# Attention beside a long convolution: four channel blocks of 128 in place of two of 256, with complex butterflies in joint operations

## The chip, the cores and the metric

The kernel runs on one core of a Trainium2 chip. The metric is the device time of one execution in microseconds (us). Engines are named as the profile names them: PE is TensorE's matrix product, PEld its weight load, DVE is VectorE, ACT is ScalarE, POOL is GpSimd, and SP is the engine that issues most DMAs.

## The reference

Two independent parts share the output (2048 rows, 512 + 512 columns). Cut to what matters:

```
def _A_ref(x, wq, wk, wv, wo):            # 32 heads of 16, one K and V for all heads, S = 2048
    q = (x @ wq).reshape(B, S, H, Dh).transpose(0, 2, 1, 3)
    k = x @ wk
    v = x @ wv
    p = softmax(einsum("bhqd,bkd->bhqk", q, k) * Dh ** -0.5)
    return einsum("bhqk,bkd->bhqd", p, v).transpose(0, 2, 1, 3).reshape(B, S, H * Dh) @ wo

def _B_ref(q, k, v, shift_k, ssm_k, ssm_D):   # 512 channels
    k_shift = sum over t of k_pad[:, t:t + S, :] * shift_k[:, ks - 1 - t]      # 4 taps
    kv = k_shift * v
    y = irfft(rfft(kv, 2 * S) * rfft(ssm_k, 2 * S))[:S]    # causal convolution for each channel
    y = y + kv * ssm_D
    return q * y

return jnp.concatenate([a, b], axis=-1)
```

## The kernel before

**What sets the order.** The Python code emits one fixed order for each engine. It keeps three clocks of its own (`pe`, `act`, `dv`) and charges every operation an assumed price; nothing is scheduled at run time. `attend` walks through 1024 *turns*. A turn is one tile of scores (L1237: eight f16 matmuls in 64x32 tiles of the array) and one exponential on ScalarE over 128x1024 (L1244). Two score tiles fit in PSUM. Every second turn TensorE multiplies two finished tiles with the values (`pv`, L1274). In the other turn `fill` may emit *units* of side work: a unit is charged 216 ns and is a 512-column f16 step or a 128-column f32 step through all eight tiles of the array (L316). As many units are emitted as fit until 380 ns after the planned start of the exponential. So the chunks have one to three units.

**Jobs.** Side work comes as jobs, the one with the earliest due turn first. A job from `pair_job` has two phases that use opposite row halves; between them GpSimd clears a small tile (`tok`, L287) for which the second phase waits, and the planner leaves 1.1 us. All jobs write one PSUM tile F, so the next may start only when VectorE has evacuated the last. Other side work are the Q projections (`xT,wq`) and the output projection (`wo,o`).

**The convolution** is a transform of 2048 points in two steps, in f32. The first step, over 128 points, is a matrix product with tables (`ff`, back with `fi`); the second, over 16, is done on VectorE by `dft16`: two radix-4 passes (`dft4`) with twiddle factors between. For each block of 256 channels there are three kinds of stage. S (`short`) forms the four-tap convolution times v on VectorE and transforms it into the spectrum `cx`. L (`long`) transposes the filter (L606), evacuates it (L612) and transforms it into `ch`. VectorE then runs `dft16` on both, multiplies them (`product`, L445) and runs `dft16` back. B (`backward`) transforms back, multiplies by q (L655) and stores. Every forward job ends in an evacuation into the spectrum (L475). `DUE` gives the due turns of the stages, whose order is S0, L0, L1, B0, S1, B1. Table tiles come in a ring of four (`FT`), 128 KB for each half tile.

**VectorE's threads.** `run_dve` emits evacuations when the planner's clock has them ready, and in between the next operation of one of several Python generators. Each `yield 1215.0` is the assumed price in ns of the operation that follows. In the twiddles of `dft16` it reads `yield 360.0` before L419 and `yield 350.0` before L421 and L423.

**DMAs** go through SP's queue, one for each turn, or two with a long list. The planner assumes 6 us to landing. Reused buffers carry real semaphores.

Of the kernel before, what the change touches and what calls it, by code (L numbers as in the profile page):

```python
# [18 lines left out]
P = 128  # L19
# [4 lines left out]
CB = 256  # L24
# [21 lines left out]
DUE = {("S", 0): (60, 150), ("L", 0): (150, 300), ("L", 1): (380, 500), ("B", 0): (500, 560), ("S", 1): (560, 660), ("B", 1): (780, 860)}  # L46
# [71 lines left out]
class _Emit:  # L118
# [247 lines left out]
    def dft4(self, x, e):  # L366
        v = self.nc.vector
        add, sub = ALU.add, ALU.subtract
        re, im = (lambda t: t[:, 0]), (lambda t: t[:, 1])
        x0, x1, x2, x3 = x  # L370
        n = 1215.0

        def both(out, a, b, op):
            for part in (re, im):
                yield n
                v.tensor_tensor(part(out), part(a), part(b), op)  # L376

        yield from both(e, x0, x2, add)
        yield from both(x2, x0, x2, sub)
        yield from both(x0, x1, x3, add)  # L380
        yield from both(x3, x1, x3, sub)
        yield n
        v.tensor_tensor(re(x1), re(x2), im(x3), add)
        yield n
        v.tensor_tensor(im(x1), im(x2), re(x3), sub)
        yield n
        v.tensor_tensor(re(x2), re(x2), im(x3), sub)
        yield n
        v.tensor_tensor(im(x2), im(x2), re(x3), add)
        yield from both(x3, e, x0, sub)  # L390
        yield from both(x0, e, x0, add)

    def dft16(self, c, first, second, sign):
        v, w = self.nc.vector, self.w
        n = c.shape[-1]
        outer = lambda i: c[:, :, 4 * i : 4 * i + 4, :]
        inner = lambda i: c[:, :, i:16:4, :]
        e = w.tile([P, 2, 4, n], F32, tag="sp", name=self.nm("sp"))
# [7 lines left out]
        for ab in ((1, 1), (1, 2), (2, 1), (1, 3), (3, 1), (2, 3), (3, 2), (3, 3), (2, 2)):  # L406
            u = w.tile([P, 2, n], F32, tag="v2", name=self.nm("u"))
            x = c[:, :, row(*ab), :]
            ang = sign * 2 * np.pi * ab[0] * ab[1] / 16
            if ab == (2, 2):  # L410
                yield 230.0
                v.tensor_copy(u[:, 0], x[:, 0])
                yield 230.0
                v.tensor_scalar(x[:, 0], x[:, 1], -float(sign), None, ALU.mult)
                yield 230.0
                v.tensor_scalar(x[:, 1], u[:, 0], float(sign), None, ALU.mult)
            else:
                yield 360.0
                v.tensor_scalar(u, x, float(np.sin(ang)), None, ALU.mult)  # L419
                yield 350.0  # L420
                v.scalar_tensor_tensor(x[:, 0], x[:, 0], float(np.cos(ang)), u[:, 1], ALU.mult, ALU.subtract)  # L421
                yield 350.0
                v.scalar_tensor_tensor(x[:, 1], x[:, 1], float(np.cos(ang)), u[:, 0], ALU.mult, ALU.add)  # L423
# [7 lines left out]
    def product(self, cx, ch):  # L431
        for i in range(4):
            r = slice(4 * i, 4 * i + 4)
            t = self.w.tile([P, 2, 4, CB], F32, tag="sp", name=self.nm("t"))
            t = t[:, 0], t[:, 1]
            for out, a, b, op in (
                (t[0], cx[:, 0, r], ch[:, 0, r], ALU.mult),
                (t[1], cx[:, 1, r], ch[:, 1, r], ALU.mult),
                (ch[:, 1, r], cx[:, 0, r], ch[:, 1, r], ALU.mult),
                (ch[:, 0, r], cx[:, 1, r], ch[:, 0, r], ALU.mult),  # L440
                (cx[:, 0, r], t[0], t[1], ALU.subtract),
                (cx[:, 1, r], ch[:, 1, r], ch[:, 0, r], ALU.add),
            ):
                yield 1215.0
# [7 lines left out]
    def spectrum(self):  # L452
        return self.w.tile([P, 2, 16, CB], F32, tag="big", bufs=2, name=self.nm("sp"))

    def tables(self):
        seq = [("ff", 0)] * 2 + [("ff", 1), ("fi", 0), ("ff", 0), ("fi", 1)]
        self.tab = []
        for kind, _ in seq:
# [7 lines left out]
    def table(self, n):  # L466
        return lambda now: len(self.tab) > n

    def forward_job(self, n, m2, c, xs, inputs, due):

        ft, h, use = self.tab[n]
        pr = [([(ft[:, rho, q, :], xs[rho]) for rho in range(2)], 256 * q, CB) for q in range(2)]

        def out(F):
            self.nc.vector.tensor_copy(  # L475
                c[:, :, 2 * m2 : 2 * m2 + 2, :].rearrange("p q m n -> p m q n"), F.rearrange("p m (q n) -> p m q n", q=2)
            )

        j = self.pair_job(pr, [(1215.0, out)], due, [h] + inputs, f32=True)
        return j, use  # L480


    def conv_pe(self):
# [4 lines left out]
        yield from self.short(0, 0)  # L488
        yield from self.long(0, 8, *self.long_load(0))
        hin = self.long_load(1)  # L490
        yield lambda now: ("p", 0) in self.seen
        yield from self.long(1, 16, *hin)
        yield lambda now: ("b", 0) in self.seen
        yield from self.short(1, 32)

    def conv_back(self):
        for blk in range(2):
            yield lambda now: ("y", blk) in self.sp
            yield from self.backward(blk, 24 + 16 * blk)

    def conv_dve(self):
        nat = [0, 1, 2, 3]
        for blk, order in enumerate((("cx", "ch"), ("ch", "cx"))):
            for n in order:
# [9 lines left out]
    def short(self, blk, tab):  # L514
        nc, v = self.nc, self.nc.vector
        cs = slice(blk * CB, (blk + 1) * CB)
        kk = self.w.tile([P, 15, CB], F32, tag="in", name=self.nm("kk"))
        nc.gpsimd.memset(kk[0:1, 0:3, :], 0.0)
        taps = self.fetch([(kk[:, 11 + i, :], self.skd[i : i + 1, cs].broadcast_to([P, CB])) for i in range(4)], self.in_free)
        edge = [(kk[a:b, i, :], self.kr[a - 1 : b - 1, 13 + i, cs]) for i in range(3) for a, b in ((1, 16), (16, P))]  # L520
        k0 = self.fetch(edge, self.in_free)
        got = {r: self.fetch([(kk[:, r + 3, :], self.kr[:, r, cs])], self.in_free) for r in range(2)}
        vs = {}

        def load(m2):
            n = self.io()
            t = self.io_tile("va", (2, 2, CB))
            r = slice(2 * m2, 2 * m2 + 2)
            vs[m2] = n, t, self.fetch([(t[:, 0, i], self.vr[:, 2 * m2 + i, cs]) for i in range(2)])
# [3 lines left out]
        ends = []  # L533
        for m2 in range(8):
            if m2 == 0:
                yield self.room(self.io_users, IO)
                load(0)
            for r in range(2 * m2 + 2, 2 * m2 + 4):
                if r < 8:
                    got[r] = self.fetch([(kk[:, r + 3, :], self.kr[:, r, cs])], self.in_free)  # L540
            for r in range(3 + 2 * m2, 5 + 2 * m2) if 1 <= m2 < 4 else range(11, 16) if m2 == 4 else ():
                got[r, 1] = self.fetch([(kk[:, r - 5, :], self.kr[:, r, cs])], ends[min(3, (r - 5) // 2)])
            if m2 < 7:
                yield self.room(self.io_users, IO)
                load(m2 + 1)
            n, t, h = vs[m2]
            seg = (lambda r: r + 3) if m2 < 4 else (lambda r: r - 5)
            need = [h, taps] + ([k0] if m2 < 2 else [])
            need += [got[r] if m2 < 4 else got[r, 1] for r in range(2 * m2 - 3, 2 * m2 + 2) if m2 >= 4 or r >= 0]
            yield self.at(*need)  # L550
            a, tmp = t[:, 1], self.w.tile([P, 2, CB], F32, tag="v2", name=self.nm("t"))
            kx = lambda i: kk[:, seg(2 * m2 - i) : seg(2 * m2 - i) + 2, :]
            tap = lambda i: kk[:, 11 + i : 12 + i, :].broadcast_to([P, 2, CB])
# [7 lines left out]
            ends.append(Stamp(self.dv))  # L561
# [3 lines left out]
            yield self.table(tab + m2)  # L565
            j, use = self.forward_job(tab + m2, m2, c, [a[:, 0], a[:, 1]], [done], self.due("S", blk, m2))
            self.users(j, self.io_users[n], use)
            jobs.append(j)
        self.in_free = ends[-1]
        self.sp["cx", blk] = c, jobs  # L570

    def users(self, j, *stamps):

        j.uses = stamps

    def long_load(self, blk):
        hin = self.w.tile([P, 2, S], F32, tag="in", name=self.nm("hin"))
        hs = []
        for ct in range(2):
            c0 = blk * CB + ct * P  # L580
            hs.append(self.fetch([(hin[:, ct, x : x + 256], self.I["B_ssm_k"][c0 : c0 + P, x : x + 256]) for x in range(0, S, 256)], self.in_free))
        return hin, hs

    def long(self, blk, tab, hin, hs):
        nc = self.nc
        yield self.at(*hs)
        for ct in range(2):
            yield 100.0
            nc.vector.tensor_add(hin[:, ct, 0:1], hin[:, ct, 0:1], self.dt[:, 2 * blk + ct : 2 * blk + ct + 1])
        ready = Stamp(self.dv)  # L590
        hv = hin.rearrange("p c (q m) -> p c m q", m=16)
        c = self.spectrum()
        jobs = []
        for m4 in range(4):
            yield self.room(self.io_users, IO)
            n = self.io()
            t = self.io_tile("hT", (4, CB))

            def turn(m, m4=m4):
                def emit(F, most):  # L600
                    if most < 2:
                        return 0, None, False
                    for i in range(2):
                        for ct in range(2):
                            x = P * ct
                            nc.tensor.transpose(F[:, m, 256 * i + x : 256 * i + x + P], hv[:, ct, 4 * m4 + 2 * m + i], self.ident)  # L606
# [7 lines left out]
            j = self.one_job([turn(m) for m in range(2)], [(1215.0, out)], self.due("L", blk, 2 * m4), [ready])  # L614
            yield self.at(j)
            for i in range(2):
                m2 = 2 * m4 + i
                yield self.table(tab + m2)
# [1057 lines left out]
```

## Time and profile before

| what | value |
|---|---|
| median of 3 runs | 1005.43 us (1002.78 to 1006.14) |
| the profiled execution | 1007.34 us, its span 1005.6 us |
| granted TensorE clock, mean | 0.986 |
| first exponential to the end of the last | 19.2 to 990.0 us |
| data moved by DMA | 85.33 MB, mean 85 GB/s |

The profiled execution is 1.9 us above the median. A row of a group reads: line, engine, operation, output <- inputs with shapes, count | busy us in all, mean ns of one | idle time of the engine just before them, and what ended it. In a row of the timeline come the start in us, the length in us, the engine, the line, the operation, the names, the count of instructions merged, and in brackets the idle time before. An f32 matmul stands in the profile as two records.

### The profile page before, as it was taken

Reading aid. Unit: us, or ns where it says so; the run is one execution under the profiler, and the core shown is the slowest. Engines: PE = TensorE matmul, PEld = TensorE weight load, DVE = VectorE, ACT = ScalarE, POOL = GpSimd, SP = SyncE. Lnnn points to the kernel's source line nnn. Section 1 sums busy time; section 2 is a strip of 40 time slices with the busy share of each in tenths; the row PEclk is TensorE's granted clock in tenths of the full one; section 3 lists DMA queues with packets and bytes.
Section 4 is the critical chain, followed back from the end, with each engine's and each line's share of the span. In section 5 each row is a group of like instructions: output and inputs, shape, how many; then the busy total and the mean of one; then the engine's idle time right before and its main releaser. Section 6 shows DMA issues by size and latency. Waiting matters only on the chain.

```text
span 1005.6 us, 53610 instructions
## 1 busy us (share of the span) xinstructions
PE 947.9 (94%) x24556; PEld 483.1 (48%) x24556; DVE 652.6 (65%) x831; ACT 960.8 (96%) x1034; POOL 43.2 (4%) x106
## 2 busy tenths in 40 slices
PE   8999999999999999899999999999888998999996
PEld 4434444554545554354555555554333443455562
DVE  4334477736894998989869945464799989111322
ACT  4799999999999999999999999999999999999993
POOL 3820000000000000000000000000000000000000
PEclk8799999999999999999999999999999999999998
DMA  7133354244024212312145333332201021331201
GB/s 223 44 108 120 111 149 138 88 128 128 24 84 118 72 36 72 86 49 73 35 123 159 93 124 103 108 100 65 66 13 52 13 61 45 94 125 54 61 5 47
DMA packets 81941, 85.33 MB, mean 85 GB/s; under 512 B 14654, under 2 KB 70312, under 8 KB 81708
## 3 DMA queue, kind: packets, MB, share of 16 engines
q1 hardware_dynamic: 80076, 81.23, 27.1%
q8 instruction: 194, 3.18, 1.3%
q10 hardware_dynamic: 1632, 0.60, 0.3%
q14 instruction: 39, 0.32, 0.1%
HBM read 56.14 MB, written 25.66 MB: 81 GB/s over the span
## 4 chain that ended last, share of the span: by engine, by line
ACT 68%; issue 14%; PE 14%; DVE 3%; DMA 1%; ACTq 0%; SPq 0%; DVEq 0%
ACT p L1244 67%; PE a L1274 5%; PE s L1237 4%; PE f L316 1%; DMA xc<-in_A_x 1%; PE b L735 1%; DMA wkvf<-in_A_wv 1%; DVE u L419 1%; DVE sp L421 1%; PE s L728 1%; PE b L775 1%; DVE sp L475 0%; PE b L772 0%; DVE sp L423 0%; PE b L748 0%
## 5 line engine op out<-in xcount | busy, mean ns | idle before, releaser
L1244 ACT ACTIVATE p<-s 128x1024 f32<-128x1024 f32 x1016 | 946.1, 1046 | 12.9 <-PE s L1237 8.1
L1274 PE MATMUL a<-p,vx 64*32 64x512 f32 (+1 forms) x8640 | 547.8, 564 | 0.2 <-issue 0.2
L1237 PE MATMUL s<-st,kst 49*32 49x512 f16 x8192 | 428.8, 383 | 43.5 <-ACT p L1244 36.1
L1237 PEld LDWEIGHTS <-kst 49*32 49x32 f16 x8192 | 198.8, 89 | 376.4 <-issue 331.6
L1274 PEld LDWEIGHTS a<-p,vx 64*32 64x32 f32 x8640 | 168.0, 106 | 24.6 <-issue 2.8
L376 DVE TENSOR_TENSOR sp<-sp 128x1024 f32<-128x1024 f32 x96 | 111.2, 1214 | 0.0
L475 DVE COPY sp<-f 128x1024 f32<-128x1024 f32 x32 | 39.2, 1224 | 87.8 <-PE f L316 87.6
L376 DVE TENSOR_TENSOR sp<-sp,sp 128x1024 f32<-128x1024 f32 x48 | 56.1, 1216 | 0.3
L316 PE MATMUL f<-wo,o 64*32 64x512 f16 x1440 | 55.3, 375 | 0.1
L1290 DVE COPY ao<-a 128x1024 f32<-128x1024 f32 x15 | 18.4, 1224 | 54.6 <-PE a L1274 54.4
L316 PE MATMUL f<-xT,wq 64*32 64x512 f16 x1344 | 51.0, 375 | 0.1
L287 POOL MEMSET tok<- 1x2 f32 x58 | 5.6, 96 | 897.8 <-PE f L316 890.0
L655 DVE TENSOR_TENSOR q<-f,q 128x1024 f32<-128x1024 f32 x8 | 9.8, 1224 | 50.8 <-PE f L316 50.8
L316 PE MATMUL f<-va,ff 64*32 64x128 f32 (+1 forms) x1472 | 41.1, 311 | 0.2
L316 PE MATMUL f<-hT,ff 64*32 64x256 f32 (+1 forms) x1344 | 41.0, 325 | 0.0
L316 PE MATMUL f<-sp,fi 64*32 64x128 f32 (+1 forms) x1424 | 40.3, 315 | 0.0
L560 DVE TENSOR_TENSOR va<-va,t 128x512 f32<-128x512 f32 x48 | 33.2, 691 | 1.5
L316 PEld LDWEIGHTS f<-va,ff 64*32 64x32 f32 x1472 | 26.8, 106 | 15.3 <-issue 3.3
L558 DVE TENSOR_TENSOR t<-kk 128x512 f32<-128x512 f32 x48 | 33.0, 687 | 1.0
L316 PEld LDWEIGHTS f<-sp,fi 64*32 64x32 f32 x1424 | 26.4, 106 | 10.2 <-issue 3.0
L316 PEld LDWEIGHTS f<-hT,ff 64*32 64x32 f32 x1344 | 24.9, 106 | 12.8 <-DVE sp L475 2.7
L316 PEld LDWEIGHTS <-o 64*32 64x32 f16 x1440 | 23.2, 93 | 15.7 <-issue 4.2
(162 smaller groups left out, 569.4 us busy)
## 6 DMA issues: line engine op xcount, KB each, us to landing
ff<-in_ff SPq DMA_DIRECT2D x64, 128.0 KB
od<-ao SPq DMA_DIRECT2D x30, 256.0 KB
qd<-qp SPq DMA_DIRECT2D x45, 128.0 KB
st<-qd SPq DMA_DIRECT2D x60, 96.0 KB
kk<-in_B_k SPq DMA_DIRECT2D x38, 128.0 KB
va<-in_B_v SPq DMA_DIRECT2D x32, 128.0 KB
hin<-in_B_ssm_k SPq DMA_DIRECT2D x32, 128.0 KB
fi<-in_fi SPq DMA_DIRECT2D x32, 128.0 KB
```

Source lines behind the costliest of these rows:

```text
L316: last = self.nc.tensor.matmul(F[32 * q : 32 * q + 32, rho, cols + a : cols + b], w[rows, 32 * q : 32 * q + 32], x[rows, a:b], start=begin ...
L376: v.tensor_tensor(part(out), part(a), part(b), op)
L419: v.tensor_scalar(u, x, float(np.sin(ang)), None, ALU.mult)
L421: v.scalar_tensor_tensor(x[:, 0], x[:, 0], float(np.cos(ang)), u[:, 1], ALU.mult, ALU.subtract)
L475: self.nc.vector.tensor_copy(c[:, :, 2 * m2 : 2 * m2 + 2, :].rearrange("p q m n -> p m q n"), F.rearrange("p m (q n) -> p m q n", q=2))
L558: v.tensor_tensor(tmp, kx(i), tap(i), ALU.mult)
L560: v.tensor_tensor(a, a, tmp, ALU.add)
L728: self.nc.tensor.matmul(out[j : j + 32], w[:, j : j + 32], x, start=start, stop=stop)
L1237: self.nc.tensor.matmul(out, self.kst[rows, c0 : c0 + 32], x, start=True, stop=True)
L1244: i = self.nc.scalar.activation(p, self.s, AF.Exp, scale=DH**-0.5 / SC / SC)
L1274: nc.tensor.matmul(out, self.vx[rows, k, :], p, start=i == 0, stop=i == NK - 1)
L1290: self.nc.vector.tensor_copy(a, self.acc)
```

## The change

The block has 128 channels (`CB`) and there are four of them. A spectrum is half as large, and three stand in SBUF in place of two, so that the next block's S stage can start before the last block's B stage has run; the order of stages is S0 L0 S1 L1 B0 S2 L2 B1 S3 L3 B2 B3. A forward job covers four rows m with two table tiles where it covered two rows with one. A backward job still covers four rows m, which are now 8 units, and fills half of F. Each stage reads its 8 tables, so 96 table tiles are loaded in place of 48. The butterflies' plain sums take the real and the imaginary part in one operation, twiddles of equal angle go in pairs, and assumed prices change. Inputs and outputs of the convolution are fetched two rows at a time, in runs of 512 B. Some tiles of the start of the attention are placed in other buffers (`in`, `big`, `px`, `wo`).

The rows below are the engines' orders, each without its row number.

On VectorE, the first spectrum `cx`, the second `dft4` pass of its forward transform (`sp` is a spectrum, or the scratch tile of the pass when it stands alone as the output; `hT`, `f` and `rl` belong to other work). Before:

```order
L376 TENSOR_TENSOR sp_5234<-sp_1456 128x1024 x2
L612 COPY hT_5798<-f_6219 128x1024
L376 TENSOR_TENSOR sp_1456<-sp_1456 128x4x256 x5
L1367 TENSOR_SCALAR rl_6042<-rl_6042 128x32
L1369 RECIPROCAL rl_6042<-rl_6042 128x32
L376 TENSOR_TENSOR sp_1456<-sp_1456 128x4x256
L475 COPY sp_5250<-f_6330 128x2x2x256
L383 TENSOR_TENSOR sp_1456<-sp_1456 128x4x256
L385 TENSOR_TENSOR sp_1456<-sp_1456 128x4x256
L387 TENSOR_TENSOR sp_1456<-sp_1456 128x4x256
L389 TENSOR_TENSOR sp_1456<-sp_1456 128x4x256
L376 TENSOR_TENSOR sp_1456<-sp_5234,sp_1456 128x4x256 x2
```

Now:

```order
L375 TENSOR_TENSOR sp_3956<-sp_1462 128x1024
L375 TENSOR_TENSOR sp_1462<-sp_1462 128x8x128 x3
L383 TENSOR_TENSOR sp_1462<-sp_1462 128x4x128 x4
L473 COPY sp_3835<-f_4681 128x2x2x256
L386 TENSOR_TENSOR sp_1462<-sp_3956,sp_1462 128x8x128 x2
L1355 TENSOR_SCALAR rl_4643<-rl_4643 128x32
L1357 RECIPROCAL rl_4643<-rl_4643 128x32
```

A pass has 16 operations of 1024 elements before; now it has six of 1024 and four of 512, and there are twice as many passes.

On TensorE, the first chunk of the first S job, three units in both versions (`va` the short convolution's result, `ff` a table, `s` scores). Before:

```order
L1237 LDWEIGHTS kst
L1237 MATMUL s_2206<-st_1014,kst 32x512
L316 MATMUL f_2215<-va_1457,ff_354 32x256 x8
L316 MATMUL f_2215<-va_1457,ff_354 32x128 x8
L1237 LDWEIGHTS kst
L1237 MATMUL s_2235<-st_1014,kst 32x512
```

Now:

```order
L1225 LDWEIGHTS kst
L1225 MATMUL s_2203<-st_1020,kst 32x512
L318 MATMUL f_2212<-va_1463,ff_360 32x128
L318 MATMUL f_2212<-va_1463,ff_361 32x128
L318 MATMUL f_2212<-va_1463,ff_360 32x128
L318 MATMUL f_2212<-va_1463,ff_361 32x128
L318 MATMUL f_2212<-va_1463,ff_360 32x128
```

The chunk keeps its three units and its place between two score tiles; its 256-column matmuls have become pairs of 128 columns, and they read two tables in turn.

On SP, the first loads of the first S stage (`kk` the keys with the taps, `skd` the taps, 15 and 112 partitions for the rows before the first). Before:

```order
L178 DMA kk_1454<-skd 128x256 x4
L178 DMA kk_1454<-in_B_k 15x256
L178 DMA kk_1454<-in_B_k 112x256
L178 DMA kk_1454<-in_B_k 15x256
L178 DMA kk_1454<-in_B_k 112x256
L178 DMA kk_1454<-in_B_k 15x256
L178 DMA kk_1454<-in_B_k 112x256
L178 DMA kk_1454<-in_B_k 128x256 x2
L178 DMA va_1457<-in_B_v 128x256 x2
```

Now:

```order
L180 DMA kk_1460<-in_B_k 128x2x128 x2
L180 DMA kk_1460<-skd 128x4x128
L180 DMA kk_1460<-in_B_k 15x3x128
L180 DMA kk_1460<-in_B_k 112x3x128
L180 DMA va_1463<-in_B_v 128x2x128 x2
```

A piece keeps its 128 KB and is cut into rows half as long; taps and edge rows come in three pieces instead of ten.

The diff, cut to its core:

```diff
-CB = 256
+CB = 128
+NB = D // CB
-DUE = {("S", 0): (60, 150), ("L", 0): (150, 300), ("L", 1): (380, 500), ("B", 0): (500, 560), ("S", 1): (560, 660), ("B", 1): (780, 860)}
+STAGES = ("S0", "L0", "S1", "L1", "B0", "S2", "L2", "B1", "S3", "L3", "B2", "B3")
+DUE = dict(zip(STAGES, (60, 110, 170, 240, 300, 340, 400, 450, 490, 550, 620, 700)))
...
     def dft4(self, x, e):
-        def both(out, a, b, op):
-            for part in (re, im):
-                yield n
-                v.tensor_tensor(part(out), part(a), part(b), op)
-        yield from both(e, x0, x2, add)
...
+        for out, a, b, op in ((e, x0, x2, add), (x2, x0, x2, sub), (x0, x1, x3, add), (x3, x1, x3, sub)):
+            yield 1215.0
+            tt(out, a, b, op)
+        for out, a, b, op in (
+            (re(x1), re(x2), im(x3), add),
+            (im(x1), im(x2), re(x3), sub),
+            (re(x2), re(x2), im(x3), sub),
+            (im(x2), im(x2), re(x3), add),
+        ):
+            yield 690.0
+            tt(out, a, b, op)
+        for out, op in ((x3, sub), (x0, add)):
+            yield 1215.0
+            tt(out, e, x0, op)
...
-        for ab in ((1, 1), (1, 2), (2, 1), (1, 3), (3, 1), (2, 3), (3, 2), (3, 3), (2, 2)):
+        for a, b in ((1, 1), (1, 2), (1, 3), (2, 3), (3, 3), (2, 2)):
+            r = sorted({row(a, b), row(b, a)})
+            n = len(r)
...
-                yield 360.0
+                yield 150.0 + 135.0 * n
                 v.tensor_scalar(u, x, float(np.sin(ang)), None, ALU.mult)
-                yield 350.0
+                yield 150.0 + 135.0 * n
                 v.scalar_tensor_tensor(x[:, 0], x[:, 0], float(np.cos(ang)), u[:, 1], ALU.mult, ALU.subtract)
...
     def spectrum(self):
-        return self.w.tile([P, 2, 16, CB], F32, tag="big", bufs=2, name=self.nm("sp"))
+        return self.w.tile([P, 2, 16, CB], F32, tag="big", bufs=3, name=self.nm("sp"))
...
-    def forward_job(self, n, m2, c, xs, inputs, due):
-        ft, h, use = self.tab[n]
-        pr = [([(ft[:, rho, q, :], xs[rho]) for rho in range(2)], 256 * q, CB) for q in range(2)]
+    def forward_job(self, n, m4, c, xs, inputs, due):
+        tabs = self.tab[n - 1 : n + 1]
+        pr = []
+        for q in range(2):
+            for i in range(2):
+                pr.append(([(tabs[rho][0][:, i, q, :], xs[2 * rho + i]) for rho in range(2)], 256 * q + CB * i, CB))
...
+        for b in range(NB):
+            if b > 1:
+                yield lambda now: ("b", b - 2) in self.seen
+            yield from self.short(b)
+            if b:
+                yield lambda now: ("p", b - 1) in self.seen
+            yield from self.long(b)
...
-            j = self.pair_job(pr, [(1215.0, out)], self.due("B", blk, b), [tabs[0][1], tabs[1][1], h, st], f32=True)
+            j = self.pair_job(pr, [(700.0, out)], self.due("B", blk, b), [tabs[0][1], tabs[1][1], h, st], f32=True)
...
     def wo_heads(self):
-        yield lambda now: self.turn >= 60
+        yield self.at(self.xdh[3])
```

243 lines of the change are left out of this document (106 added, 137 removed).

## The prediction

> **What bounds the kernel now.** I read the page's busy line and its chain first, then the exponentials alone in order of time, then the stages.
>
> ```profile
> PE 947.9 (94%) x24556; PEld 483.1 (48%) x24556; DVE 652.6 (65%) x831; ACT 960.8 (96%) x1034; POOL 43.2 (4%) x106
> ...
> ACT 68%; issue 14%; PE 14%; DVE 3%; DMA 1%; ACTq 0%; SPq 0%; DVEq 0%
> ...
> L1244 ACT ACTIVATE p<-s 128x1024 f32<-128x1024 f32 x1016 | 946.1, 1046 | 12.9 <-PE s L1237 8.1
> ```
>
> ScalarE is busy 96% of the span with one kind of instruction, the 1024 exponentials of L1244, and they hold 68% of the chain. TensorE is close behind, VectorE is not (65%). The change touches no exponential, so it can pay or cost only through the distance from one exponential to the next. By stage (columns: stretch, then busy us and count of PE, PEld, DVE, ACT, POOL, then clock, DMA share, GB/s):
>
> ```profile
> 19.00:93.00 74.00, 72.36 (x1216) 32.53 (x1208) 29.21 (x59) 62.52 (x64) 33.38 (x34) 0.86 0.25 79
> ...
> 725.00:775.00 50.00, 40.28 (x872) 16.74 (x879) 47.59 (x64) 50.00 (x56) 0.00 (x0) 1.00 0.12 32
> ...
> 990.00:1005.60 15.60, 6.53 (x80) 2.14 (x64) 4.57 (x11) 0.00 (x0) 0.00 (x0) 0.76 0.11 39
> ```
>
> ```profile
> 93.00:990.00 897.00, 853.48 (x23168) 439.79 (x23161) 609.55 (x746) 891.36 (x961) 7.24 (x61) 1.00 0.28 82
> ```
>
> The start (64 exponentials in 74 us, TensorE busy 72 of it) and the end (15.6 us after the last one) belong to attention alone. The stretch between is where the convolution lies: 897 us, ScalarE busy 891. The exponentials there, merged wherever one follows the other without a gap (start, length, count, the gap before):
>
> ```profile
> 92.41 27.16 ACT L1244 ACTIVATE p<-s 128x1024 f32<-128x1024 f32 x29
> 119.81 59.26 ACT L1244 ACTIVATE p<-s 128x1024 f32<-128x1024 f32 x64 [0.23 <-PE f L316]
> 179.24 62.28 ACT L1244 ACTIVATE p<-s 128x1024 f32<-128x1024 f32 x67 [0.17 <-PE f L316]
> 241.72 41.38 ACT L1244 ACTIVATE p<-s 128x1024 f32<-128x1024 f32 x44 [0.20 <-PE s L1237]
> 283.58 186.38 ACT L1244 ACTIVATE p<-s 128x1024 f32<-128x1024 f32 x200 [0.48 <-PE s L1237]
> 470.73 68.34 ACT L1244 ACTIVATE p<-s 128x1024 f32<-128x1024 f32 x73 [0.78 <-PE s L1237]
> 539.27 59.36 ACT L1244 ACTIVATE p<-s 128x1024 f32<-128x1024 f32 x64 [0.20 <-ACT p L1244]
> 598.81 305.85 ACT L1244 ACTIVATE p<-s 128x1024 f32<-128x1024 f32 x330 [0.18 <-ACT p L1244]
> 905.47 70.53 ACT L1244 ACTIVATE p<-s 128x1024 f32<-128x1024 f32 x76 [0.82 <-PE s L1237]
> 976.50 13.47 ACT L1244 ACTIVATE p<-s 128x1024 f32<-128x1024 f32 x14 [0.50 <-PE s L1237]
> ```
>
> 961 exponentials in 897.56 us: 0.934 us each. The nine gaps sum to 3.56 us. The same view in a stage without any convolution or projection unit, and in a dense one:
>
> ```profile
> 725.09 48.85 ACT L1244 ACTIVATE p<-s 128x1024 f32<-128x1024 f32 x53
> ```
>
> ```profile
> 619.09 71.66 ACT L1244 ACTIVATE p<-s 128x1024 f32<-128x1024 f32 x77
> ```
>
> The last one of a row lasts its 1.05 us (the mean of L1244), so the pitch is (48.85 - 1.05)/52 = 0.919 without units and (71.66 - 1.05)/76 = 0.929 with them. At 0.919 throughout, 960 pitches would take 882.5 us: all that any placement of side work could give back is 897.6 - 1.05 - 882.5 = 14.0 us, gaps included.
>
> **The change, part by part.** TensorE. Each of the three kinds of stage has 128 units in both versions (a unit: 128 columns in f32 through all eight 64x32 tiles): 384 in all. Before, 119 pairs of units ran as one 256-column matmul and 146 units as 128 columns; now all 384 run as 128. What a 128-column unit costs:
>
> ```profile
> 514.55 0.65 PE L316 MATMUL f<-sp,fi 64*32 64x128 f32 x32
> 514.99 0.43 PE L1237 MATMUL s<-st,kst 49*32 49x512 f16 x8
> 515.21 0.86 PE L316 MATMUL f<-sp,fi 64*32 64x128 f32 x32
> ```
>
> Start to start: 32 records (two units, each matmul recorded twice) in 0.44 us, 0.22 a unit, and the eight f16 matmuls behind them 0.22. [...] The weights that are now loaded twice as often are hidden: 0 us.
>
> ```profile
> L316 PEld LDWEIGHTS f<-sp,fi 64*32 64x32 f32 x1424 | 26.4, 106 | 10.2 <-issue 3.0 <-DVE q L655 0.6 <-DVE sp L475 0.3
> ```
>
> [...]
>
> How the units fall between the scores is counted in the order: chunks of three units 119 before and 122 now, of two 138 and 124, of one 68 and 86, alternate gaps without any 100 and 94; the eight-matmul transposes 16 and 16. Up to turn 117 the chunks are the same. So the pitch stays: 0 us by count. The one shift is in place: stretches of 32 turns with 34 units or more go from eight to four, and the three without any go.
>
> VectorE. The rows for its forms:
>
> ```profile
> L376 DVE TENSOR_TENSOR sp<-sp 128x1024 f32<-128x1024 f32 x96 | 111.2, 1214 | 0.0
> ...
> L560 DVE TENSOR_TENSOR va<-va,t 128x512 f32<-128x512 f32 x48 | 33.2, 691 | 1.5
> ...
> L419 DVE TENSOR_SCALAR u<-sp 128x512 f32<-128x512 f32 x48 | 20.4, 426 | 1.4
> L421 DVE SCALAR_TENSOR_TENSOR sp<-sp,u 128x256 f32<-128x256 f32 x48 | 20.4, 425 | 1.6
> ...
> L412 DVE COPY u<-sp 128x256 f32<-128x256 f32 x6 | 1.8, 294 | 0.2
> ...
> L1491 DVE TENSOR_SCALAR lr<-lr 128x16 f32<-128x16 f32 x2 | 0.4, 185 | 0.1
> ```
>
> - Butterflies: 192 x 1.214 = 233 us before; 144 x 1.214 + 96 x 0.691 = 241 now: +8. Joining the two parts keeps 1024 elements in an operation, since the block is half as wide, and the four mixed ones shrink to 512 and keep their fixed cost.
> - Twiddles: 48 x (0.426 + 2 x 0.425) + 18 x 0.294 = 66.5; now 36 such triples (45.9), 24 scalings of 256 elements (7.1), and 84 operations of 128 elements, which the trace lacks. They lie between 0.185 (16 elements) and 0.425 (256); I take 0.30, nearest to the 256-element copy: 25.2. Together 78.2: +12, with ends +2 and +22.
> - Product: 48 x 1.214 = 58.3; now 16 x 1.214 + 64 x 0.691 = 63.7: +5. Output multiplies: 8 x 1.224 against 16 x 0.691: +1. Short convolution, evacuations and transposed filters keep form and count.
>
> VectorE gets 26 us more (17 to 37). [...]
>
> What hides it: VectorE has 897 - 610 = 287 us idle in the long stretch. 0 us, as long as no TensorE job stands behind a late evacuation. Before, some did:
>
> ```profile
> 280.91 0.29 DVE L412 COPY u<-sp 128x256 f32<-128x256 f32 x1
> 281.12 1.22 DVE L475 COPY sp<-f 128x1024 f32<-128x1024 f32 x1
> ...
> 282.39 0.72 PE L606 MATMUL f<-ident,hin 128*128 128x128 f32 x4 [0.50 <-DVE sp L475]
> ...
> 283.58 2.10 ACT L1244 ACTIVATE p<-s 128x1024 f32<-128x1024 f32 x2 [0.48 <-PE s L1237]
> ```
>
> The evacuation of the only F tile came late between twiddles, the transposes waited 0.50 us, the scores behind them on TensorE too, and ScalarE lost 0.48. The planner charges a triple 360 + 350 + 350 = 1060 ns and the trace shows 1276; eight a transform, so it believes VectorE 1.7 us earlier than it is. The new code charges 3 x 420 for the same triple. I let this gap and the like one of 0.78 at 470.73 go: -1.3 us. What is late next there is the transposes' own work, which is unchanged.
>
> Jobs: backward has 16 jobs of 8 units for 8 of 16, so 8 more changes of phase (a memset on GpSimd, then the opposite rows) and 8 more evacuations. The planner keeps 1.1 us between phases; the gaps above name no GpSimd: 0 us, ends 0 and 8 x 0.63 = +5 (the mean of the two late evacuations).
>
> Loads: 96 table pieces more and 14 pieces fewer, 82 issues more on SP. Rows of k, v, q and the output are 512 B for 1 KB, bytes unchanged; the tables add 96 x 128 KB = 12.6 MB.
>
> ```profile
> 125.00:150.00 25.00, 22.95 (x636) 11.73 (x635) 18.07 (x25) 24.98 (x28) 0.18 (x2) 1.00 0.52 146
> ```
>
> ```profile
> q1 hardware_dynamic: 80076, 81.23, 27.1%
> ```
>
> ```profile
> L178 SPq DMA_DIRECT2D kk<-in_B_k x50: 312/329/1067, 90.5 to 649.0; - x50
> ```
>
> 82 x 0.33 = 27 us of SP's queue over the whole span, and 12.6/81.2 of 27.1% is 4 points of DMA share where the busiest stretch has 52%: 0 us. A table now blocks a job in pairs; behind a matmul that waits for one stand the next scores, so a late table would cost as the transposes did. The chain gives all DMA 1%.
>
> Sum: 1007.34 - 1.3 = 1006.0 for a profiled execution; that one lies 1.9 us above the median, so on the median 1005.43 - 1.3 = 1004.1 us.
>
> **The rivals.**
> - *Thinner stages pay* (faster). All nine gaps go (3.6 us), and four dense stretches of 32 turns fall from 0.936, as the next row has it ((30.07 - 1.05)/31), to 0.919: 4 x 32 x 0.017 = 2.2 us. That makes 999.6. Against it: three-unit chunks are no fewer, and two gaps name ScalarE itself.
>
> ```profile
> 867.20 30.07 ACT L1244 ACTIVATE p<-s 128x1024 f32<-128x1024 f32 x32
> ```
>
> - *VectorE hands the F tile back late more often* (slower). 26 us more on VectorE and 8 more jobs through one F tile. Each late return costs 0.5 to 0.8 us; from five net on it is more than 3 us, at eight 1005.4 + 5.0 = 1010.4. For it: VectorE fills 47.6 of 50 us in some stages. Against it: the corrected charges.
> - *Weight loads show* (slower). If each pass of a 128-column unit waited for a load (0.106 us by the PEld row, two passes), the 238 units that were paired cost 0.21 more each, 50 us; TensorE idles 43.5 us in the long stretch, so 6 to 50 us come through, some 1033. The 0.22 us a unit speaks against it. [...]
>
> **How the numbers follow.** About 0.3% (3.0 us) can be told from no change here. My forecast, 0.61; thinner stages 0.20; late returns 0.16; weight loads 0.03. So faster 0.20, same 0.61, slower 0.19. The range takes in the first rival and nearly the second: 999.5 to 1010.
>
> **What would show it.** Right: VectorE near 679 us; the f32 units still 0.22 us; gaps between exponentials near 2 us in sum; pitch near 0.92 to 0.93 everywhere, without the empty stage. Wrong: more gaps that name TensorE's F jobs or a table's DMA, an extra wait at the start, or a pitch that moves in all stages at once.

## The result, and the profile after

The changed kernel takes 1015.72 us (median of 4 runs, 1013.34 to 1018.57) beside 1004.6 us for the kernel before (4 runs): ratio 1.010, 95% interval 1.0078 to 1.0121. The forecast was 1004.1 us with a range from 999.5 to 1010; the kernel became 11 us slower, so the forecast was wrong. The profiled execution has 1015.61 us and a span of 1013.8 us, 8.2 us more than before's.

From the page after: the busy line, the queue of instruction packets (packets, MB, share of 16 engines), the chain, and the exponentials.

```profile
PE 955.0 (94%) x26460; PEld 512.7 (51%) x26460; DVE 674.9 (67%) x973; ACT 964.4 (95%) x1034; POOL 43.9 (4%) x116
...
q8 instruction: 209, 3.42, 1.5%
...
ACT 58%; PE 29%; issue 12%; DVE 1%; ACTq 0%; DVEq 0%
...
L1232 ACT ACTIVATE p<-s 128x1024 f32<-128x1024 f32 x1016 | 949.8, 1043 | 17.2 <-PE s L1225 11.6
```

TensorE's share of the chain went from 14% to 29%, although it is busy 94% as before and its matmuls became no slower (a 128-column f32 matmul of L318 lasts 271 ns on average, where L316 had 268 to 269). The exponentials wait 17.2 us where they waited 12.9, 11.6 of it for scores (8.1 before). The same queue in the page before:

```profile
q8 instruction: 194, 3.18, 1.3%
```

TensorE has 2 x 24,556 = 49,112 records before (matmuls and weight loads) and 2 x 26,460 = 52,920 now: 3808 more. These are the 119 pairs of units that were one 256-column matmul and are two now, at 32 records a unit. The instruction queue has 15 packets more; 3808/15 is 254, and 3.42 MB/209 is 16 KB. So a packet is a block of about 256 TensorE instructions.

The exponentials in order of time, merged where no gap lies between (start, length, count, the gap before; six rows of the stretch behind 93 us):

```profile
534.50 4.85 ACT L1232 ACTIVATE p<-s 128x1024 f32<-128x1024 f32 x5 [1.09 <-PE s L1225]
539.55 81.39 ACT L1232 ACTIVATE p<-s 128x1024 f32<-128x1024 f32 x87 [0.20 <-ACT p L1232]
...
734.05 90.61 ACT L1232 ACTIVATE p<-s 128x1024 f32<-128x1024 f32 x97 [0.97 <-PE s L1225]
825.20 33.83 ACT L1232 ACTIVATE p<-s 128x1024 f32<-128x1024 f32 x36 [0.54 <-PE s L1225]
...
910.01 33.55 ACT L1232 ACTIVATE p<-s 128x1024 f32<-128x1024 f32 x36 [1.14 <-PE s L1225]
...
992.14 6.52 ACT L1232 ACTIVATE p<-s 128x1024 f32<-128x1024 f32 x7 [1.07 <-PE s L1225]
```

Behind 93 us there are 20 gaps of 9.4 us in sum, where before had nine of 3.56: 5.8 us more. Exponentials that follow one another overlap by 0.11 us (1.043 long, 0.933 apart), so the 11 additional gaps cost 1.2 us beyond their length: 7.0 us together. From the start of the 65th exponential to that of the last it is 906.1 us now and was 895.6, which is 10.5 us more. (The spans differ by less because the 65th comes 1.8 us earlier in this execution; in the traces of the variants below it lies anywhere from 90.2 to 94.8 us.) The other 3.5 us lie between the gaps, where the mean distance of two exponentials, the pitch, went from 0.929 to 0.933; the long rows above have (81.39 - 1.05)/86 = 0.934 and (90.61 - 1.05)/96 = 0.933. So two thirds of the time are lost in few places. One of them, in TensorE's timeline:

```profile
530.91 1.05 PE L1262 MATMUL a<-p,vx 64*32 64x512 f32 x16
531.77 0.41 PE L1225 MATMUL s<-st,kst 49*32 49x512 f16 x8
532.01 0.39 PE L318 MATMUL f<-xT,wq 64*32 64x512 f16 x2
533.33 0.83 PE L318 MATMUL f<-xT,wq 64*32 64x512 f16 x22 [0.93 <-issue]
533.79 0.59 PE L1225 MATMUL s<-st,kst 49*32 49x512 f16 x8
```

TensorE stops after the second matmul of a job whose inputs have long been there, and it waits for nothing that the profile shows ("issue"). In the trace an instruction packet ran from 530.88 to 531.95, and TensorE went on at 533.33, 1.4 us behind its end. The same holds at the other large gaps: the packet ends 1.2 to 1.5 us before TensorE goes on, and the stops lie whole blocks of 256 records apart, up to the few records that a trace misses. (At some of them the weight loads show the stop better: ahead of the gap at 910.01 us they stand still for 1.29 us, to 908.60, while the three matmul records ahead last until 908.23 and leave TensorE 0.38 idle.) Of the 20 gaps 16, with 8.4 of the 9.4 us, follow such a stop by less than 1.5 us. This gave the theory: *TensorE's instructions arrive in blocks of 256, and in dense stretches of short matmuls it has used a block up before the next is there.* A pair of turns holds 32 instructions for two score tiles, 32 for the product with the values and 32 for each f32 unit of 128 columns: 160 in about 1.9 us with a chunk of three units.

Every one of the 209 packets moved 16,384 bytes, and the streams below break at every 128 matmuls with their 128 loads, which agrees with that size. In the trace of the streams the first stop comes after 449 of TensorE's records and ahead of any packet; how far ahead of TensorE the blocks arrive was not shown.

### The profile page after: what moved, and what is told of

It is laid out like the page before. It is cut to its first block, busy times and chain, and to the rows that moved or that the text cites. A ratio compares the mean times of both kernels' runs of the same rounds, so it can differ in the third digit from the quotient of the medians.

```text
span 1013.8 us, 57767 instructions
## 1 busy us (share of the span) xinstructions
PE 955.0 (94%) x26460; PEld 512.7 (51%) x26460; DVE 674.9 (67%) x973; ACT 964.4 (95%) x1034; POOL 43.9 (4%) x116
## 3 DMA queue, kind: packets, MB, share of 16 engines
q8 instruction: 209, 3.42, 1.5%
## 4 chain that ended last, share of the span: by engine, by line
ACT 58%; PE 29%; issue 12%; DVE 1%; ACTq 0%; DVEq 0%
ACT p L1232 57%; PE a L1262 11%; PE s L1225 7%; PE f L318 6%; PE b L847 1%; PE b L722 1%; PE b L715 1%; PE s L715 1%; PE b L765 0%; PE b L762 0%; PE b L735 0%; DVE wp L1422 0%; ACT held L1232 0%; ACT xT L856 0%; DVE y L1509 0%
## 5 line engine op out<-in xcount | busy, mean ns | idle before, releaser
L1232 ACT ACTIVATE p<-s 128x1024 f32<-128x1024 f32 x1016 | 949.8, 1043 | 17.2 <-PE s L1225 11.6
L1225 PE MATMUL s<-st,kst 49*32 49x512 f16 x8192 | 444.8, 381 | 42.9 <-ACT p L1232 35.9
L383 DVE TENSOR_TENSOR sp<-sp 128x512 f32<-128x512 f32 x96 | 60.2, 682 | 0.6
L318 PE MATMUL f<-wo,o 64*32 64x512 f16 x1440 | 57.9, 375 | 0.3 <-issue 0.3
L318 PE MATMUL f<-xT,wq 64*32 64x512 f16 x1344 | 51.9, 375 | 0.9 <-issue 0.9
L318 PE MATMUL f<-sp,fi 64*32 64x128 f32 x2048 | 48.9, 271 | 0.8 <-issue 0.4
L318 PE MATMUL f<-hT,ff 64*32 64x128 f32 x2048 | 46.1, 271 | 0.7 <-issue 0.6
L318 PE MATMUL f<-va,ff 64*32 64x128 f32 x2048 | 45.8, 271 | 0.0
L318 PEld LDWEIGHTS f<-sp,fi 64*32 64x32 f32 x2048 | 39.8, 106 | 11.1 <-issue 4.3
L318 PEld LDWEIGHTS f<-hT,ff 64*32 64x32 f32 x2048 | 37.7, 106 | 11.0 <-issue 3.5
L318 PEld LDWEIGHTS f<-va,ff 64*32 64x32 f32 x2048 | 38.7, 106 | 8.7 <-issue 3.4
L638 DVE TENSOR_TENSOR q<-f,q 128x512 f32<-128x512 f32 x16 | 11.0, 690 | 41.8 <-PE f L318 40.9
L550 DVE TENSOR_TENSOR va<-va,tm 128x512 f32<-128x512 f32 x48 | 33.2, 692 | 1.5
```

Of the source, the lines that this page charges most:

```text
L318: last = self.nc.tensor.matmul(F[32 * q : 32 * q + 32, rho, cols + a : cols + b], w[rows, 32 * q : 32 * q + 32], x[rows, a:b], start=begin ...
L383: tt(out, a, b, op)
L550: v.tensor_tensor(a, a, tmp, ALU.add)
L638: nc.vector.tensor_tensor(x, F[:, :, 0 : 2 * CB], x, ALU.mult)
L1225: self.nc.tensor.matmul(out, self.kst[rows, c0 : c0 + 32], x, start=True, stop=True)
L1232: i = self.nc.scalar.activation(p, self.s, AF.Exp, scale=DH**-0.5 / SC / SC)
```

## The experiments

Ratios are to the kernel before, run beside each on the same chip. The gaps are those behind 93 us in the profiled execution, from the view used above.

| kernel | TensorE records | gaps: count, us | median us | ratio, 95% |
|---|---|---|---|---|
| before | 49,112 | 9, 3.6 | 1005 | |
| after | 52,920 | 20, 9.4 | 1015.7 | 1.0078 to 1.0121 |
| before, matmuls cut | 53,048 | 26, 13.6 | 1021.5 | 1.0140 to 1.0189 |
| cut, at most two f32 units | 53,048 | 19, 10.2 | 1015.4 | 1.0054 to 1.0122 |
| after, at most two f32 units | 52,920 | 13, 5.1 | 1008.2 | 1.0008 to 1.0038 |
| after, half a block later | 53,048 | 19, 7.5 | 1011.7, one run | |
| after, a sharper cap | 52,856 | 14, 6.7 | 1020.7 | 1.0122 to 1.0166 |
| after, tiles of 64 columns | 46,584 | 6, 1.9 | 1034.8 | 1.0277 to 1.0331 |
| before, tables loaded twice | 49,112 | 11, 3.9 | 1006.1 | 1.0001 to 1.0028 |
| before, whole matmuls | 46,840 | 7, 3.1 | 1004.4 | 0.9970 to 1.0001 |
| the same, twiddles priced | 46,936 | 4, 1.1 | 1002.8 | 0.9961 to 0.9995 |

**The one part alone: cut before's matmuls.**

```diff
+ for e, f in [(e, e + P) for e in range(a, b, P)] if f32 else [(a, b)]:
-     matmul(F[.., cols + a : cols + b], w[..], x[rows, a:b], start=begin, ..)
+     matmul(F[.., cols + e : cols + f], w[..], x[rows, e:f], start=begin and e == a, ..)
```

> The kernel before, with each f32 matmul of 256 columns emitted as two of 128: 119 of them per tile, so 119 x 32 = 3808 more TensorE instructions (49,112 to 52,920, the count of the kernel after), with the columns, VectorE, the DMAs and the order of all stages as before. Theory (TensorE's instructions are fetched in blocks of 256, and a stretch of dense f32 units uses them up faster than blocks arrive): more gaps between exponentials that name TensorE, each at the end of an instruction block, and 1009 to 1016 us, most of the change's 11 us. Rival A (the 12.6 MB more of tables in 512-byte rows): 1004.5 us, no change. Rival B (VectorE's 22 us more and eight more hand-overs of tile F): 1004.5 us, no change. Rival C (where the new order puts its chunks): 1004.5 us.

1021.48 us, 16 us more, above the theory's 1016 and far from every rival's 1004.5. The edit also cut four pairs in the last projection (`wl,lr`), hence 3936 instructions more and not 3808. VectorE is as before, 652.5 us:

```profile
PE 956.2 (94%) x26524; PEld 515.6 (50%) x26524; DVE 652.5 (64%) x831; ACT 966.6 (95%) x1034; POOL 43.1 (4%) x106
```

```profile
536.75 8.52 ACT L1245 ACTIVATE p<-s 128x1024 f32<-128x1024 f32 x9 [1.32 <-PE s L1238]
...
918.34 2.85 ACT L1245 ACTIVATE p<-s 128x1024 f32<-128x1024 f32 x3 [1.43 <-PE s L1238]
```

TensorE at the first of these:

```profile
533.95 0.63 PE L317 MATMUL f<-sp,fi 64*32 64x128 f32 x22
536.00 0.32 PE L317 MATMUL f<-sp,fi 64*32 64x128 f32 x5 [1.41 <-issue]
```

It stops in the middle of a chunk, with tables and spectrum there. So the number of matmuls is enough to make the kernel slower, with no new order, loads or VectorE work. What else the change does gives some 6 us of the 16 back (1.0100 against 1.0164, intervals apart). Which part does was not separated; the dense stretches of 32 turns, eight before and four now, fit.

**The cost by itself: streams of small products.** Added behind the warm-up of the kernel before:

```diff
+ for x, cols, units in ((zf, 128, 96), (zf, 256, 96), (z, 512, 192), (z, 32, 192), (zf, 128, 96)):
+     for i in range(units):
+         for q in range(4):
+             for r in range(2):
+                 rows = slice(64 * r, 64 * r + 64)
+                 matmul(b[r][32*q : 32*q+32, 0:cols], x[rows, 32*q : 32*q+32], x[rows, 0:cols], start=True, stop=True)
```

> The kernel before, with five streams of small products of a zero tile added behind the warm-up, each of 3072 TensorE instructions (12 blocks of 256) in 64x32 tiles that wait for nothing: 96 f32 units of 128 columns, 96 of 256 columns, 192 f16 units of 512 columns, 192 of 32 columns, and the first again. The columns alone take 96 x 0.22 = 21 us, 42, 41, about 3, and 21 us. Theory (a block of 256 instructions takes at least 3.7 us to arrive): 44 us for every stream, whatever its columns, with stalls of TensorE at every block in the first, fourth and last. Without that bound: 21, 42, 41, 10 to 20, 21 us. The total is some 150 to 220 us longer, which says nothing by itself.

TensorE's timeline, from the first stream, the second, the fourth and the fifth:

```profile
15.73 3.66 PE L866 MATMUL b<-zf 64*32 64x128 f32 x128 [4.56 <-issue]
...
58.11 40.52 PE L866 MATMUL b<-zf 64*32 64x256 f32 x1458 [0.37 <-issue]
...
148.58 1.22 PE L866 MATMUL b<-z 64*32 64x32 f16 x128 [2.54 <-issue]
152.58 1.22 PE L866 MATMUL b<-z 64*32 64x32 f16 x128 [2.78 <-issue]
156.31 1.22 PE L866 MATMUL b<-z 64*32 64x32 f16 x128 [2.51 <-issue]
159.76 1.22 PE L866 MATMUL b<-z 64*32 64x32 f16 x128 [2.23 <-issue]
...
188.22 2.02 PE L866 MATMUL b<-zf 64*32 64x128 f32 x128 [0.65 <-issue]
191.67 2.02 PE L866 MATMUL b<-zf 64*32 64x128 f32 x128 [1.44 <-issue]
195.13 2.02 PE L866 MATMUL b<-zf 64*32 64x128 f32 x128 [1.44 <-issue]
199.13 2.02 PE L866 MATMUL b<-zf 64*32 64x128 f32 x128 [1.99 <-issue]
```

The streams of 128-column f32 and of 32-column matmuls break into pieces of exactly 128 matmuls and 128 loads. In the fourth and the fifth stream a piece starts 3.45 to 4.00 us after the one before, whether its matmuls take 1.22 us or 2.02; over the eleven from 188.22 to the last start at 228.45 it is 40.23/11 = 3.66 us on average. The five streams take 47, 43, 44, 43 and 44 us, near the 44 of the forecast for each: the last for work of 21, while the 256-column stream hardly stops (its row lacks the first 77 of its 1536 matmuls). So where these streams ran at a DMA share of 0.02, 256 instructions cost 3.5 to 4.0 us or the time of their columns, whichever is more.

**Half a block later.** The kernel after, with 64 small matmuls (128 instructions) in the warm-up:

```diff
+ for i in range(64):
+     matmul(b[i % 2][:, 0:32], z[:, 0:P], z[:, 0:32], start=True, stop=True)
```

> The kernel after, with 64 small matmuls (128 instructions, 32 columns each) added to the warm-up ahead of everything, so that every later TensorE instruction stands half a block of 256 later. Nothing else is changed. Theory (instruction fetch): the gaps between exponentials keep their number and sum within a half (5 to 15 us) but stand at other turns than in the kernel after, half a block away, each still where a block of 256 ends; time 1010 to 1020 us. Rivals A, B and C: the gaps stay at the same turns, since the loads, VectorE's operations and the order are the same.

1011.7 us in the one run, and 7.5 us of gaps, both as forecast. Three rows of its exponentials:

```profile
822.59 33.65 ACT L1234 ACTIVATE p<-s 128x1024 f32<-128x1024 f32 x36 [0.43 <-PE s L1227]
...
907.02 10.44 ACT L1234 ACTIVATE p<-s 128x1024 f32<-128x1024 f32 x11 [0.93 <-PE s L1227]
918.49 60.35 ACT L1234 ACTIVATE p<-s 128x1024 f32<-128x1024 f32 x65 [1.03 <-PE s L1227]
```

Counted in exponentials, the gaps behind the 843rd, 879th and 932nd now lie behind the 844th, 880th and 933rd; those at 535, 746, 968 and 972 are gone, and new ones stand at 686, 717 and 944, among others. The stop ahead of the gap at 910.01 us in the kernel after comes behind 47,230 of TensorE's records, and the one ahead of the gap at 907.02 us here behind 47,486: a whole block of 256 apart, though every instruction stands only 128 later. So the stops keep to the blocks and not to the work. The attention's work, its order and the loads are the same. A late table or a late F tile would not move with the number of instructions ahead of it.

**The same instructions, spread thinner.**

```diff
+ if j.f32:
+     left = min(left, 2 - done)
- took, last, over = items[self.at_phase](self.F, left)
+ took, last, over = items[self.at_phase](self.F, left) if left > 0 else (0, None, False)
```

> The kernel after, with at most two f32 units in a chunk where there were up to three: the same 52,920 instructions, VectorE's work and DMAs, only spread thinner. A pair of turns with a chunk of three f32 units holds 160 instructions in about 1.9 us, with two 128. Theory (a stretch of dense f32 units uses blocks of 256 instructions up faster than one each 3.7 us): most gaps that end with a block go, 1004 to 1010 us. Rival D (each added instruction has its own price wherever it stands, 11 us / 3808 = 2.9 ns): 1013 to 1018 us. Rivals B (VectorE's hand-overs of F) and C: 1012 to 1020 us.

1008.23 us: of the 1.0% remain 0.23% (0.08 to 0.38), with all the instructions, loads, VectorE operations and hand-overs of the kernel after. So here density, not count, set the price. As far as the cap brings nothing else, what VectorE, jobs and loads cost without dense chunks is bounded by that 0.23%, and gaps at block ends still have a part in it (the largest 0.80 us). The pitch between the gaps is back at 0.929.

The same cap on the kernel before with cut matmuls:

> The kernel before with its f32 matmuls cut to 128 columns (52,920 TensorE instructions) and at most two f32 units in a chunk. Cutting alone gave 1021.5 us. Theory (density against the arrival of blocks): most of the 16 us comes back, 1005 to 1011 us. If the count of instructions itself were paid for, or the cut matmuls ran longer: 1018 to 1024 us.

1015.37 us: 6 of the 16 us came back, not most. This forecast missed. The stages of before are denser, and chunk after chunk of two units is 256 instructions in 3.7 us, right at the measured time of a block:

```profile
549.67 7.68 ACT L1249 ACTIVATE p<-s 128x1024 f32<-128x1024 f32 x8 [0.55 <-PE s L1242]
558.26 7.68 ACT L1249 ACTIVATE p<-s 128x1024 f32<-128x1024 f32 x8 [0.91 <-PE s L1242]
567.05 55.37 ACT L1249 ACTIVATE p<-s 128x1024 f32<-128x1024 f32 x59 [1.10 <-PE s L1242]
```

A gap comes every eight turns, two blocks. In the trace the packets there start at 555.51, 558.92, 564.12 and 567.77: every second one comes 4.9 or 5.2 us behind the last, and TensorE stands still until 1.4 us after its end. Why single packets start that late is not settled here: from the end of one packet to the start of the next the DMA share was 0.67 and 0.33 ahead of the late ones, and 0.33 and 0.51 ahead of the others.

**More tables for before.** Each table piece loaded a second time into one tile that nobody reads:

```diff
  i = self.nc.sync.dma_start(x[4], x[5])
+ if tuple(x[4].shape) == (P, 2, P):
+     self.dep(self.nc.sync.dma_start(self.spare[0], x[5]), self.last_exp)
```

> The kernel before, with each piece of a table loaded a second time, into one spare tile that nobody reads: 96 more loads of 128 KB, 12.6 MB more, about what the change adds (12.07 MB). TensorE's instructions stay 49,112. Theory (instruction fetch): within 0.3% of 1005 us, as the number of instruction packets is the same and the queues have room. Rival A (the added loads hold up data or the instruction packets): 1008 to 1016 us.

```profile
q1 hardware_dynamic: 93900, 93.82, 31.1%
```

12.6 MB more cost 0.14% (0.01 to 0.28). By themselves the loads are no main cause; what they cost is at the edge of what can be told. Added to the denser blocks of the kernel after they were not tested.

**Tiles of 64 columns for after's f32 units.**

```diff
- for q in range(4):            # 32 columns of the array each
+ z = 64 if f32 else 32
+ for q in range(P // z):       # F[z*q : z*q+z], w[rows, z*q : z*q+z]
```

> The kernel after, with its f32 side work in tiles of 64 rows x 64 columns of the array in place of 64 x 32: half as many matmuls and loads for the same columns, the order of the stages, VectorE and the DMAs as in the kernel after. Some 6,000 to 7,000 fewer TensorE instructions of 52,920. Theory (instruction fetch): a unit is then 16 instructions as an f16 unit is, no stretch is denser than about 110 a pair of turns, the gaps that end on an instruction block go, and the time falls to 1001 to 1005 us. Rivals A (DMA), B (VectorE and hand-overs) and C (order): 1013 to 1016 us, as the kernel after.

1034.77 us, the worst of all, against the theory's 1001 to 1005. Yet the gaps went, as the theory wants: after 117 us there are rows as long as

```profile
116.97 245.16 ACT L1233 ACTIVATE p<-s 128x1024 f32<-128x1024 f32 x256 [0.34 <-PE f L319]
```

The pitch of this row is (245.16 - 1.02)/255 = 0.957, and the mean between all gaps is 0.962, where after has 0.933: 0.0295 x 953 = 28 us, of which the 14 gaps that went give 9 back (7.5 us of length and 14 x 0.11). That leaves the measured 19 us. TensorE's timeline shows where it goes; first this kernel, then the kernel after:

```profile
218.30 0.41 PE L1226 MATMUL s<-st,kst 49*32 49x512 f16 x8
218.65 0.67 PE L319 MATMUL f<-hT,ff 64*64 64x128 f32 x16
219.24 0.41 PE L1226 MATMUL s<-st,kst 49*32 49x512 f16 x8
```

```profile
216.61 0.41 PE L1225 MATMUL s<-st,kst 49*32 49x512 f16 x8
216.82 0.64 PE L318 MATMUL f<-hT,ff 64*32 64x128 f32 x32
217.27 0.42 PE L1225 MATMUL s<-st,kst 49*32 49x512 f16 x8
```

From a score tile to the first matmul of the chunk it is 0.35 us in place of 0.21, and two units take 0.59 in place of 0.45. So the gain in instructions was more than lost, as far as this chunk shows, to tiles of another shape between those of 64x32. Whether the switch or the shape itself costs it was not separated.

**A better version.** The rule turned round: before's 256-column matmuls are cut only where a chunk would stay empty (4 of 146 short units are left).

```diff
+ whole = getattr(items[self.at_phase], "left", lambda: 1)()
+ if whole > left and done:
+     break
```

> The kernel before, with its 256-column f32 matmuls cut in two only where a chunk would otherwise stay empty: 6 pairs of 128-column units are left of 73, so about 67 x 32 = 2144 fewer TensorE instructions (47,000 in place of 49,112), with the same columns, loads and VectorE's work. Theory (arrival of instruction blocks): the kernel before lost about 2 us to such gaps itself (at 905.5 and behind 970 us), and they go: 1001 to 1004 us. If before was not limited in this way, or the units that a chunk now leaves empty are missed later: 1005 to 1009 us.

1004.43 us, ratio 0.9986 (0.9970 to 1.0001): the gap at 905 us is gone, and with 1.0001 the interval does not exclude no change. Then, on top, the twiddles' assumed prices:

```diff
- yield 230.0
+ yield 300.0
...
- yield 360.0
+ yield 390.0
...
- yield 350.0
+ yield 390.0
```

> The kernel before with whole 256-column matmuls (1004.4 us, 0.9986 of before) and with the assumed prices of the twiddles nearer to the 0.42 us and 0.29 us that they take (390 and 300 ns in place of 360, 350 and 230), so that the planner sends fewer transposes into the queue before VectorE has evacuated F. Theory: the two gaps that this left (0.56 and 0.80 us) shrink, 1002 to 1004.5 us, under the kernel before by more than the interval. If such waits are hidden by later slack: 1004.4 us again. TensorE's instructions stay at about 47,000.

1002.79 us, ratio 0.9978 (0.9961 to 0.9995): faster than both kernels, by little. Its exponentials run from 77 to 535 us in one row:

```profile
77.05 457.93 ACT L1247 ACTIVATE p<-s 128x1024 f32<-128x1024 f32 x491 [0.59 <-PE s L1240]
```

A sharper cap on the kernel after went the other way:

```diff
- left = min(left, 2 - done)
+ left = min(left, min(2, 5 - self.prev_f32 - self.prev_prev) - done)   # f32 units of the two chunks before
```

> The kernel after, with at most two f32 units in a chunk and at most five in three chunks that follow one another, so that long dense stretches stay under 256 instructions in 3.7 us; the convolution ends later in the attention than with the cap of two alone (1008.2 us). Theory: the four gaps of 0.6 to 0.8 us that the cap of two left go, 1002 to 1007 us; against it works that the last jobs end nearer to the last exponential, which would show as a longer tail (15.1 us in the kernel after). If the remaining 3 us over the kernel before are VectorE's or the loads': 1007 to 1010 us.

1020.69 us, where the theory had 1002 to 1007. The gaps at block ends did not go: at the two largest until 950 us, 0.64 us at 904.17 and 0.58 at 926.85, the weight loads stand still for 0.70 and 0.63 us, marked "issue", and go on 1.4 and 1.3 us behind the end of a packet. And the convolution's last jobs were pushed to the end: the last exponential ends at 992.97, and the span at 1022.5, a tail of 29.5 us where after has 15.1.

```profile
964.41 28.56 ACT L1245 ACTIVATE p<-s 128x1024 f32<-128x1024 f32 x31 [0.16 <-PE s L1238]
```

```profile
999.27 3.79 PE L330 MATMUL f<-wl,lr 64*32 64x256 f32 x80 [3.99 <-issue]
```

The last projection, TensorE's row above, starts 6.3 us behind the last exponential.

## Why the prediction was wrong, step by step

- **The step that failed** is the first term, "The weights that are now loaded twice as often are hidden: 0 us". It priced a unit from a chunk that ran freely, two in 0.44 us, and that price held: two units still take 0.45 us (216.82 to 217.27 above). What the loads add by themselves was not separated. What was not priced is the number of instructions. The cut alone, 3936 more of them, cost 16 us in the kernel before, more than the whole loss of the kernel after. The rival on weight loads was not this: it expected every paired unit to grow by 0.21 us, and where TensorE does not stop they did not.
- **The sign that was there.** The page before already had its share. At the gap of 0.82 us at 905.47, which the prediction counted among nine and did not explain, the weight loads stand still and go on 1.5 us behind the end of an instruction packet (902.64):

```profile
904.10 0.12 PEld L1274 LDWEIGHTS a<-p,vx 64*32 64x32 f32 x3 [0.92 <-issue]
```

  This gap was gone once the matmuls were left whole. It is also missing in the trace with the tables loaded twice, where TensorE's instructions are those of before, so one gap in one trace proves little by itself.
- **The pitch, 0 us by count of chunks.** It rose from 0.929 to 0.933 between the gaps, 3.5 us over the stretch; the cap of two units brings it back to 0.929. Whether short stops at block ends make this part was not separated. The spread of dense stages, a rival there, may be what gives back up to 6 us (that was not separated either), but only against a cost that the same change brings.
- **VectorE, +26 us, hidden.** It rose by 22.3 us, to 674.9 (679 forecast). The 128-element forms, taken at 0.30 us, have 0.23 to 0.29:

```profile
L417 DVE SCALAR_TENSOR_TENSOR sp<-sp,u 128x128 f32<-128x128 f32 x24 | 7.0, 291 | 0.8
...
L408 DVE COPY u<-sp 128x128 f32<-128x128 f32 x12 | 2.7, 227 | 0.4
```

- **Late evacuations, -1.3 us.** Right in kind: both gaps are gone. The transposes' waits for VectorE's evacuations, from before and from after (us in all, times, longest):

```profile
PEld f L606 <- DVE sp L475: 3.4, 5, 1.3
```

```profile
PEld f L585 <- DVE sp L473: 0.7, 2, 0.4
```

  The corrected prices alone moved the whole-matmul version from 0.9986 to 0.9978, in the right direction and within both intervals.
- **Eight more jobs, 0 us.** No gap of after names GpSimd, or VectorE. The rival of late F tiles (1010.4 us) is nearest to the measured time but has the wrong cause: cutting matmuls alone, with before's jobs, was slower still.
- **Loads, 0 us.** 0.14% (0.01 to 0.28) shows when only they are added to the kernel before; that they make the blocks of the kernel after come later is possible and not shown.
- **"What would show it"** named "more gaps that name TensorE's F jobs" as a sign of being wrong, and near 2 us of gaps as a sign of being right. They came, 9.4 us of them, though most name the scores, which are what TensorE does next.

## What to carry to other kernels

Count the instructions of a dense stretch as well as its columns: here, one block after another, 256 TensorE instructions, loads included, did not pass in less than 3.5 to 4.0 us, so by an estimate from the streams a matmul with its load must bring about 29 ns of columns to pay for itself (3.66 us / 128; an f32 matmul counts as two records). Cutting a matmul in two at the same column time was free here only where TensorE did not stop at a block's end (two units in 0.45 us); the sign of such a stop was the mark "issue" in the middle of a ready job, at the matmuls (0.93 us at 533.33 in the kernel after) or at the weight loads (1.29 us at 908.60). Thin out dense chunks (1008.2 us for 1015.7) or keep matmuls long (1004.4 us), and see that neither another tile shape (1034.8 us) nor a later end (1020.7 us) eats the gain.

## What the runs showed of the hardware that was not expected

- A block's time did not follow TensorE's granted clock. The streams of 32 columns and the last one ran at granted clocks of 0.53 and 0.97 (first fence: stretch, then busy us and count of PE, PEld, DVE, ACT, POOL, then clock, DMA share, GB/s), and a block took 3.45 to 4.00 us in both.
- Beside other DMA traffic a block took longer. In the streams, the one that began at 15.73 us lasted until 21.93, 6.2 us, at a DMA share of 0.72 (second fence), although its matmuls took 3.7; the next, at a share of 0.01, took 4.0. In the kernel after, the block ahead of the gap of 1.09 us lasted from 528.23 to 533.33, 5.1 us, and the one ahead of the last gap from 987.43 to 991.18, 3.75 us; from the start of each block to the end of the packet that TensorE then waited for, the share was 0.66 and 0.03 (third fence). Without the 0.93 us of the stop the first of these would have taken 4.2 us, so in the middle of the kernel a stretch can stop that uses its blocks up more slowly than the streams could. That the instruction packets wait behind the data is the likely reading; no run tests it by itself.

```profile
144.85:185.10 40.25, 13.73 (x1454) 12.60 (x1453) 0.00 (x0) 0.00 (x0) 0.00 (x0) 0.53 0.02 4
185.15:229.40 44.25, 25.54 (x1555) 22.14 (x1546) 0.00 (x0) 0.00 (x0) 0.00 (x0) 0.97 0.02 4
```

```profile
15.70:21.90 6.20, 3.66 (x128) 3.33 (x128) 0.00 (x0) 0.00 (x0) 2.09 (x2) 0.50 0.72 189
21.90:25.90 4.00, 3.67 (x128) 3.32 (x128) 0.00 (x0) 0.00 (x0) 2.05 (x2) 0.50 0.01 4
```

```profile
528.23:531.95 3.72, 3.70 (x136) 2.31 (x128) 1.22 (x2) 3.72 (x5) 0.00 (x0) 1.00 0.66 181
987.43:989.82 2.39, 2.39 (x112) 2.08 (x120) 0.00 (x0) 1.90 (x3) 0.00 (x0) 1.00 0.03 7
```
